# Transposes in two 64-row halves, w_out loaded in row order, and a new written-out order, in a fused attention and gated linear unit kernel

## The chip, the cores and the metric

The kernel runs on one core of one Trainium2 chip. A core has TensorE (PE: matmuls and transposes, which write to PSUM), VectorE (DVE), ScalarE (ACT), GpSimd (POOL) and SyncE (SP), which here does little but issue DMAs. The metric is the device time of one launch in microseconds. Before the change it is 201.42 us, the median of 3 runs (200.97 to 202.28).

## The reference

Inputs are q, k and v of 8 batches x 8 heads x 576 positions x 64, and three weights: w_val and w_out (512 x 512) and conv_w (5 x 512), all in float32. The output is 8 x 576 x 512 in float32.

```python
# attention, causal in blocks of 64
scores = (1/8) * q @ k.T
scores = where(block_i >= block_j, scores, -1e9)      # block = position // 64
attn = softmax(scores) @ v
x = attn.transpose(0, 2, 1, 3).reshape(8, 576, 512)   # heads side by side
# gated linear unit with a causal convolution over 5 positions
gate = sigmoid(sum_k conv_w[k] * x[:, s - 4 + k, :])
out = (gate * (x @ w_val)) @ w_out
```

## The kernel before

**Units of work.** Heads go in pairs: p = 0 to 31 is a pair of heads of one batch, four pairs a batch. A head's 576 positions are cut in 512 and a tail of 64; the tails of a batch's eight heads are loaded and turned together. For each pair:

- lq, lk, lv load q, k and v (v in one DMA for each head) as float32; cq and cv cast them to fp16, nearly always on POOL.
- T turns q and k: eight TensorE transposes of 128 x 128 into one PSUM bank; Te copies them to SBUF and puts the positions in order. lt, ct, TT and TTe do this for a batch's tails, and lvt, cvt load and cast the tails of v.
- S computes transposed scores in three pieces, t = 0, 1, 2. Each matmul has 64 rows (the size of a head), the two heads on different halves of the array, into two banks. E is the exponential on ACT, 128 x 1024 elements for each piece. mka and mkb clear the blocks that causality forbids, on POOL. SL and EL are the last tail's own scores, once a batch.
- A is attn times v, 30 matmuls of 128 rows and 65 columns (the 65th gives the sum); N divides by the sum on DVE.
- X turns the result, five transposes of 128 x 128, and Xe copies it to SBUF, so that a batch's x lies with its features on the partitions.

For each half batch n = 0 to 15, C is the convolution in 80 matmuls of 32 x 32, CS its tanh on ACT (a sigmoid in another form), V is x times w_val and Ve multiplies the two on DVE. For two batches u together, O projects 128 positions with w_out (t = 0 to 8), Oe copies a tile of the output to SBUF and Od stores it. The very last tile is done in two halves, OL, OLe, OLd.

**The weights.** w_val is cast with its columns permuted so that the features of V's output fall where the convolution's do. w_out has to match: lwo loads it, cwo casts it, W moves its rows in groups of 32 between partitions with 16 matmuls against a folded identity, and We copies them back with a factor of 0.5. CW turns conv_w with fp32 matmuls; CWe makes of it the diagonals that C uses.

**The order.** Nothing is scheduled by a compiler. The string PLAN (lines 12 to 101) lists all operations as name/indices/engine/bank, and the loop at its end issues them in this order. Each engine works through its own part of the list strictly in order, waiting on semaphores where an operand or a buffer isn't ready. S and G are the SP and POOL queues, P, V and A are TensorE, VectorE and ScalarE. So a load behind another load or an output store in PLAN is issued behind it, and a TensorE operation that has to wait holds all behind it.

**Buffers.** There are 5 tiles for loaded q and k and 5 for v, 4 each for cast and turned q and k, 5 for cast v, 4 for the exponentials, 6 for output tiles. PSUM's eight banks are three pairs (0 to 2: S, SL, A, C, V) and two single banks (3 and 4: T, TT, X, O and others). `mm` (line 127) records all matmuls, `copy` (lines 192 and 194) all copies and casts, so these lines gather many operations in the profile. Transposes are at line 322 (q and k), 354 (tails) and 453 (X).

Of the kernel before, what the change touches and what calls it, by code (L numbers as in the profile page):

```python
# [12 lines left out]
lk/1/S pact//A ppool//G lq/1/S lk/0/A lq/0/S lt/0.1/S pdve//V cq0/1/A w0/14/P/4 cq/1/G lt/0.0/S  # L13
lk/2/S lcv//S lq/2/S T/1/P/2 cq/2/G Te/1/A lq/3/S cq0/0/V lk/3/S S/1.0/P/2 lvt/0/S T0/1/P/3 E/1.0/A
T0e/1/V S/1.1/P/1 T0/0/P/0 lk/4/S T0e/0/A E/1.1/A lt/1.0/S lt/1.1/S S/0.1/P/0 cq/3/V lq/4/S ct/0/G
E/0.1/A S/0.0/P/1 TT/0/P/2 lv/0.0/S TTe/0/V E/0.0/A T/2/P/3 lv/0.1/S lq/5/S S/0.2/P/0 SL/0/P/2
Te/2/V S/1.2/P/1 T/3/P/4 Te/3/V lk/5/S lv/1.1/S CW//P/3 lv/1.0/S cvt/0/G cv/0/V E/0.2/A lk/6/S
lq/6/S E/1.2/A S/2.1/P/0 lv/3.1/S mka/0/G S/2.2/P/1 lvt/1/S ct/1/G TT/1/P/4 lv/2.0/S lv/3.0/S EL/0/A
mkb/1/G E/2.1/A S/3.0/P/2 CWe//V cq/4/G mkb/0/G A/0/P/0 TTe/1/V E/2.2/A N/0/V S/3.1/P/1 T/4/P/4
cq/5/G S/2.0/P/0 mka/1/G cv/1/G E/3.0/A E/3.1/A T/5/P/3 mkb/2/G lv/2.1/S cq/6/G S/3.2/P/1 E/2.0/A  # L20
Te/4/V lv/4.1/S mka/3/G E/3.2/A Te/5/V A/1/P/2 SL/1/P/0 S/4.1/P/1 EL/1/A T/6/P/3 N/1/V mka/2/G
cv/2/V lk/7/S S/4.0/P/0 X/0/P/4 cvt/1/G lwo/1/S mkb/3/G cv/3/G lv/4.0/S Te/6/V E/4.1/A S/4.2/P/2
E/4.0/A mka/4/G A/2/P/1 A/3/P/0 lwo/0/S E/4.2/A S/5.1/P/2 cwo/1/G N/2/V X/2/P/3 lq/7/S S/5.0/P/1
lv/5.0/S cv/4/G lv/5.1/S mkb/4/G Xe/0/A lwv/0/S lwv/1/S N/3/V E/5.1/A cq/7/G Xe/2/V lv/6.0/S
S/5.2/P/0 lv/6.1/S cv/5/G E/5.0/A X/3/P/4 Xe/3/V E/5.2/A X/1/P/3 lq/8/S A/4/P/2 lk/8/S Xe/1/V lk/9/S
N/4/V mkb/5/G C/0/P/1+0 CS/0.1/A T/7/P/3 S/6.0/P/2 X/4/P/4 lq/9/S CS/0.0/A lt/2.0/S S/6.2/P/0
cwo/0/G Te/7/V lt/2.1/S Xe/4/V E/6.0/A cwv/1/V lv/7.1/S S/6.1/P/1 E/6.2/A mka/5/G lv/7.0/S W/1/P/3
cwv/0/G E/6.1/A mka/6/G A/5/P/2 mkb/6/G We/1/A V/0.0/P/0 cv/6/G N/5/V cq/8/G cq/9/G S/7.1/P/1
W/3/P/3 W/2/P/4 Ve/0.0/V E/7.1/A lvt/2/S S/7.2/P/0 A/6/P/2 lk/11/S E/7.2/A S/7.0/P/1 ct/2/G W/0/P/0
lv/8.1/S We/2/V cv/7/G We/3/V lq/11/S E/7.0/A T/8/P/3 X/5/P/4 mka/7/G N/6/V Te/8/A lt/3.1/S lv/8.0/S  # L30
lk/10/S C/1/P/1+2 We/0/V S/8.1/P/0 Xe/5/V mkb/7/G TT/2/P/4 CS/1.0/A cq/11/G X/6/P/3 lq/10/S CS/1.1/A
V/0.1/P/1 E/8.1/A TTe/2/V lt/3.0/S Ve/0.1/V S/8.0/P/2 lv/12.0/S T/9/P/4 Xe/6/V E/8.0/A A/7/P/0
mka/8/G S/8.2/P/2 lk/12/S SL/2/P/1 O/0.0/P/3 Te/9/V O/0.1/P/4 EL/2/A E/8.2/A lq/13/S N/7/V cvt/2/G
lv/10.0/S S/9.1/P/0 S/9.2/P/1 mkb/8/G Oe/0.1/V Oe/0.0/A X/7/P/3 E/9.1/A Xe/7/V lv/11.1/S V/1.0/P/2
lv/9.1/S cv/8/G lv/9.0/S E/9.2/A Ve/1.0/V A/8/P/0 ct/3/G S/9.0/P/1 E/9.0/A T/11/P/3 lv/10.1/S
cq/10/G lt/4.1/S Te/11/A mkb/9/G T/10/P/4 lt/4.0/S N/8/V C/2/P/0+2 Te/10/V V/1.1/P/1 CS/2.0/A
lq/12/S S/10.0/P/0 Ve/1.1/V lt/5.1/S CS/2.1/A cv/9/G lq/16/S S/10.1/P/2 E/10.0/A lk/13/S E/10.1/A
TT/3/P/4 mka/9/G TTe/3/V lk/14/S S/10.2/P/1 mka/10/G cv/10/G O/0.3/P/3 E/10.2/A mkb/10/G lv/11.0/S
A/9/P/0 S/11.0/P/2 Oe/0.3/V lk/16/S N/9/V E/11.0/A S/11.1/P/1 lv/14.0/S cq/12/G O/0.2/P/4 A/10/P/0
lq/14/S lk/17/S Oe/0.2/V lv/13.0/S cq/13/G S/11.2/P/2 lq/15/S cv/11/G lv/12.1/S N/10/V T/12/P/3  # L40
lvt/4/S X/8/P/4 E/11.1/A C/3/P/1+0 E/11.2/A mkb/11/G cq/14/G Xe/8/A mka/11/G SL/3/P/2 CS/3.0/A
lvt/3/S Te/12/V EL/3/A CS/3.1/A X/10/P/4 Od/0.1/S lt/5.0/S T/13/P/3 V/2.1/P/1 lv/13.1/S S/12.1/P/2
Xe/10/V Te/13/V V/2.0/P/0 Ve/2.1/V V/3.0/P/1 X/9/P/4 lk/15/S Ve/2.0/V Ve/3.0/V E/12.1/A lv/15.0/S
lv/16.1/S A/11/P/0 S/12.0/P/2 lk/18/S N/11/V S/12.2/P/1 E/12.0/A cv/12/G Od/0.0/S E/12.2/A ct/4/G
O/0.5/P/3 cvt/3/G V/3.1/P/0 Xe/9/V TT/4/P/4 lk/19/S Oe/0.5/V T/14/P/3 S/13.0/P/2 Ve/3.1/V mkb/12/G
TTe/4/A E/13.0/A S/13.1/P/1 lv/15.1/S X/11/P/0 Od/0.2/S Te/14/V mka/12/G lv/16.0/S E/13.1/A
O/0.4/P/4 A/12/P/2 cq/15/G Oe/0.4/A Xe/11/V N/12/V cv/13/G S/13.2/P/0 S/14.0/P/1 mka/13/G O/0.6/P/3
T/15/P/4 E/14.0/A C/4/P/1+2 Oe/0.6/V E/13.2/A mkb/13/G X/12/P/3 cq/16/G CS/4.1/A A/13/P/0 SL/4/P/2
CS/4.0/A EL/4/A Te/15/V lv/14.1/S S/14.2/P/1 N/13/V lq/17/S E/14.2/A lv/18.1/S T/16/P/4 Xe/12/V
S/14.1/P/2 cv/14/G V/4.0/P/0 Ve/4.0/V E/14.1/A lvt/5/S mkb/14/G cv/15/G mka/14/G lq/18/S S/15.2/P/1  # L50
lq/20/S O/0.7/P/3 Oe/0.7/V Od/0.4/S E/15.2/A lv/17.1/S cvt/4/G Te/16/A lv/18.0/S A/14/P/0 S/15.1/P/2
E/15.1/A S/15.0/P/1 cq/17/G T/17/P/3 lq/19/S N/14/V E/15.0/A X/14/P/4 lt/6.1/S C/5/P/0+2 Te/17/V
S/16.1/P/1 O/0.8/P/3 lv/17.0/S cv/16/G CS/5.0/A CS/5.1/A mka/15/G mkb/15/G A/15/P/0 E/16.1/A cv/17/G
N/15/V cv/18/G V/4.1/P/2 Oe/0.8/A cq/18/G Xe/14/A X/13/P/3 lk/20/S Ve/4.1/V S/16.0/P/1 lq/21/S
S/16.2/P/0 lk/21/S E/16.0/A E/16.2/A ct/5/G X/15/P/4 V/5.0/P/2 Xe/15/V T/18/P/4 lt/6.0/S Od/0.3/S
S/17.0/P/1 Ve/5.0/V Xe/13/V mka/16/G lk/22/S mkb/16/G S/17.2/P/0 E/17.2/A A/16/P/2 E/17.0/A
O/1.1/P/3 lq/22/S S/17.1/P/0 N/16/V C/6/P/1+2 E/17.1/A mkb/17/G CS/6.0/A Oe/1.1/V lv/21.0/S
lv/20.1/S CS/6.1/A cq/19/G Te/18/V TT/5/P/3 V/5.1/P/0 S/18.1/P/1 Ve/5.1/V Od/0.7/S cq/22/G lv/19.0/S
lq/23/S S/18.2/P/2 lk/23/S cq/20/G lv/19.1/S TTe/5/A O/1.0/P/4 mka/17/G lv/22.0/S E/18.1/A Oe/1.0/V
T/19/P/0 E/18.2/A lv/20.0/S lv/21.1/S A/17/P/1 S/18.0/P/2 T/20/P/4 cq/21/G N/17/V X/16/P/3 Te/19/A  # L60
Te/20/V E/18.0/A lk/25/S Od/0.6/S ct/6/G SL/5/P/0 EL/5/A S/19.0/P/1 cvt/5/G V/6.0/P/2 S/19.2/P/0
mka/18/G mkb/18/G E/19.0/A Ve/6.0/V X/17/P/4 E/19.2/A lq/25/S S/19.1/P/1 Xe/16/V A/18/P/2 cv/20/G
E/19.1/A T/21/P/3 N/18/V lv/22.1/S cv/19/G Te/21/A C/7/P/0+1 CS/7.1/A lq/27/S V/6.1/P/2 lt/7.1/S
T/22/P/3 mkb/19/G S/20.1/P/1 CS/7.0/A Xe/17/V S/20.0/P/0 Ve/6.1/V E/20.1/A E/20.0/A S/20.2/P/2
Te/22/V E/20.2/A O/1.3/P/4 Od/0.5/S V/7.0/P/1 O/1.2/P/3 mka/19/G mka/20/G Oe/1.3/A lk/24/S lq/26/S
S/21.0/P/0 lv/25.0/S cq/25/G cv/21/G E/21.0/A lv/24.0/S Ve/7.0/V Oe/1.2/V lv/24.1/S S/21.2/P/1
# [38 lines left out]
def kernel(  # L105
# [32 lines left out]
    def consts(n, shape, dt, tag):  # L138
        return [const(shape, dt, f"{tag}_{i}") for i in range(n)]


    PP = [psum.tile([128, 2 if i < 3 else 1, 512], fp32, tag=f"P{i}", name=f"P{i}")
          for i in range(5)]

    def one(b):
        return PP[b][0:128, 0]

# [461 lines left out]
```

## Time and profile before

| what | us |
|---|---|
| median of 3 runs | 201.42 |
| the profiled execution: span, first to last instruction | 199.25 |
| TensorE busy | 184.3 |
| ScalarE busy | 139.4 |
| VectorE busy | 121.3 |
| GpSimd busy | 85.3 |
| last matmul ended | 195.6 |

The page gives only the span of the profiled execution; the time of a run also holds what lies around it, some 2.2 us if that execution was a median one. Times on the page are counted from the span's start. Busy time is the union of an engine's instructions. A matmul's recorded duration is its latency, so several overlap; the distance between starts tells what each costs. The loads and stores move 40.42 MB in 70,336 packets, of which 48,149 are under 512 bytes. The core's 16 DMA engines and the granted TensorE clock have rows of their own, 40 slices of about 5 us each.

### The profile page before, as it was taken

Reading aid. Unit: us, or ns where it says so; the run is one execution under the profiler, and the core shown is the slowest. Engines: PE = TensorE matmul, PEld = TensorE weight load, DVE = VectorE, ACT = ScalarE, POOL = GpSimd, SP = SyncE. Lnnn points to the kernel's source line nnn. Section 1 sums busy time; section 2 is a strip of 40 time slices with the busy share of each in tenths; the row PEclk is TensorE's granted clock in tenths of the full one; section 3 lists DMA queues with packets and bytes.
Section 4 is the critical chain, followed back from the end, with each engine's and each line's share of the span. In section 5 each row is a group of like instructions: output and inputs, shape, how many; then the busy total and the mean of one; then the engine's idle time right before and its main releaser. Section 6 shows DMA issues by size and latency. Waiting matters only on the chain.

```text
span 199.3 us, 8575 instructions
## 1 busy us (share of the span) xinstructions
PE 184.3 (92%) x3706; PEld 129.3 (65%) x3706; DVE 121.3 (61%) x193; ACT 139.4 (70%) x172; POOL 85.3 (43%) x201
## 2 busy tenths in 40 slices
PE   6389999699999799999999999999996999999992
PEld 3248677457676677767777776767764766676651
DVE  5047687675676676764666666777655383664562
ACT  3476896749779638798799888679694888643221
POOL 7255656763635535366394084282606041210000
PEclk9855899879999999999999999999999999999999
DMA  5999999999989999999969819991277610421445
GB/s 183 213 230 274 212 272 342 300 187 243 231 171 271 259 217 315 257 236 290 255 159 278 211 38 303 250 293 62 96 199 227 122 56 3 161 104 68 155 154 215
DMA packets 70336, 40.42 MB, mean 203 GB/s; under 512 B 48149, under 2 KB 64789, under 8 KB 70298
## 3 DMA queue, kind: packets, MB, share of 16 engines
q1 hardware_dynamic: 69882, 39.48, 77.6%
q8 instruction: 29, 0.48, 1.1%
q10 hardware_dynamic: 416, 0.39, 0.6%
q14 instruction: 9, 0.07, 0.1%
HBM read 30.42 MB, written 9.44 MB: 200 GB/s over the span
## 4 chain that ended last, share of the span: by engine, by line
PE 75%; DMA 9%; ACT 4%; POOL 4%; issue 3%; DVE 2%; SPq 1%; POOLq 0%; DVEq 0%; ACTq 0%
PE P L127 64%; PE P L322 7%; PE P L453 4%; DMA vs<-in_v_dram 3%; ACT pt L388 3%; DMA vts<-in_v_dram 3%; DMA qks<-in_q_dram 2%; PE P L354 1%; POOL qk L194 1%; DVE x L445 1%; ACT qkT L192 1%; POOL v16t L194 1%; POOL v L194 1%; POOL w_out L194 1%; POOL pt L410 0%
## 5 line engine op out<-in xcount | busy, mean ns | idle before, releaser
L388 ACT ACTIVATE pt<-P 128x1024 f16<-128x1024 f32 x96 | 93.7, 1025 | 24.0 <-PE P L127 22.9
L194 POOL CAST qk<-qks 128x1024 f16<-128x1024 f32 x30 | 31.0, 1043 | 15.4 <-DMA qks<-in_q_dram 10.9
L127 PE MATMUL P<-xt,w_val 128*128 128x288 f16 x256 | 37.3, 291 | 0.0
L127 PEld LDWEIGHTS <-pt 128*128 128x128 f16 x960 | 32.8, 99 | 5.9 <-issue 1.6
L127 PE MATMUL P<-v,pt 128*128 128x65 f16 x896 | 34.5, 196 | 1.9 <-POOL pt L410 0.9
L127 PE MATMUL P<-w_out,gv 128*128 128x512 f16 (+1 forms) x148 | 36.0, 374 | 0.0
L512 DVE SCALAR_TENSOR_TENSOR gv<-th,P 128x576 f16<-128x576 f32 x32 | 24.1, 752 | 18.9 <-PE P L127 15.0
L127 PE MATMUL P<-qkT 64*128 64x256 f16 (+3 forms) x256 | 31.8, 316 | 2.8 <-ACT qkT L192 1.8
L194 DVE COPY qkT<-P 128x1024 f16<-128x1024 f16 (+1 forms) x23 | 27.3, 1196 | 4.1 <-PE P L322 3.9
L127 PEld LDWEIGHTS <-w_val 128*128 128x128 f16 x256 | 23.8, 99 | 8.2 <-issue 1.1
L494 ACT ACTIVATE th<-P 128x576 f32<-128x576 f32 x32 | 19.2, 648 | 12.8 <-PE P L127 12.8
L127 PEld LDWEIGHTS <-qkT 64*128 64x128 f16 x512 | 17.0, 97 | 16.8 <-issue 10.0
L445 DVE TENSOR_TENSOR x<-P,rc 128x640 f16<-128x640 f32 x32 | 26.4, 824 | 1.1
L194 DVE COPY osb<-P 128x512 f32<-128x512 f32 x28 | 19.1, 688 | 10.4 <-PE P L127 8.3
L410 POOL MEMSET pt<- 64x256 f16 x32 | 9.8, 306 | 31.8 <-ACT pt L388 31.1
L322 PE MATMUL P<-ident,qk 128*128 128x128 f16 x256 | 20.8, 228 | 2.6 <-POOL qk L194 2.6
L444 DVE RECIPROCAL rc<-P 128x10 f32<-128x10 f32 x32 | 7.0, 220 | 25.0 <-PE P L127 23.7
L194 POOL CAST v<-vs 128x512 f16<-128x512 f32 x30 | 18.4, 619 | 8.3 <-DMA vs<-in_v_dram 5.0
L322 PEld LDWEIGHTS <-qk 128*128 128x128 f16 x256 | 16.1, 102 | 7.1 <-POOL qk L194 3.4
L127 PEld LDWEIGHTS <-gv 128*128 128x128 f16 x148 | 12.6, 98 | 12.2 <-issue 1.3
L127 PE MATMUL P<-xt,DG 32*32 32x288 f16 x1280 | 16.9, 288 | 0.0
L416 POOL MEMSET pt<- 64x128 f16 x32 | 6.5, 204 | 22.8 <-ACT pt L388 22.1
(57 smaller groups left out, 154.4 us busy)
## 6 DMA issues: line engine op xcount, KB each, us to landing
out_dram<-osb SPq DMA_DIRECT2D x35, 256.0 KB, 3.1
qks<-in_q_dram SPq DMA_DIRECT2D x32, 256.0 KB, 5.3
vs<-in_v_dram SPq DMA_DIRECT2D x64, 128.0 KB, 5.1
qks<-in_k_dram SPq DMA_DIRECT2D x31, 256.0 KB, 5.1
tls<-in_k_dram SPq DMA_DIRECT2D x8, 128.0 KB, 5.9
tls<-in_q_dram SPq DMA_DIRECT2D x8, 128.0 KB, 6.1
vts<-in_v_dram SPq DMA_DIRECT2D x8, 128.0 KB, 5.5
w_out_st<-in_moe_w_out_dram SPq DMA_DIRECT2D x2, 512.0 KB, 6.4
```

The source lines that it names most:

```text
L127: nc.tensor.matmul(out=out, lhsT=lhsT, rhs=rhs, start=start, stop=stop, skip_group_check=True)
L192: nc.scalar.copy(out=out, in_=in_)
L194: (nc.vector if eng == "V" else nc.gpsimd).tensor_copy(out=out, in_=in_)
L322: nc.tensor.transpose(out=r[:, o:o + 128], in_=t[0:128, c, 2 * i:2 * i + 2, 0:64], identity=ident16[0:128, 0:128])
L388: nc.scalar.activation(out=rot(pts, p)[0:128, 0:2, 512 * t:512 * t + 512], in_=PP[where.pop(("S", p, t))][0:128], func=AF.Exp, bias=0.0, s ...
L410: nc.gpsimd.memset(pt[64:128, 0:2, 0:1024].rearrange("p h (t s) -> p h t s", t=2)[:, :, :, 0:64], 0.0)
L416: nc.gpsimd.memset(rot(pts, p)[64:128, 0:2, 1024:1088], 0.0)
L444: nc.vector.reciprocal(out=rc[0:128], in_=r[:, :, :, 64:65])
L445: nc.vector.tensor_tensor(out=rot(x16, p)[0:128].rearrange("p i h d -> p h i d"), in0=r[:, :, :, 0:64], in1=rc[0:128].to_broadcast([128, 2 ...
L453: nc.tensor.transpose(out=half16(bank)[:, 128 * i:128 * i + 128], in_=rot(x16, p)[0:128, i, 0:2, 0:64], identity=ident16[0:128, 0:128])
L494: nc.scalar.activation(out=rot(ths, n)[0:128, 2 * i:2 * i + 2, 0:288], in_=PP[where["C", n][i]][0:128, 0:2, 0:288], func=AF.Tanh, bias=0.0 ...
L512: nc.vector.scalar_tensor_tensor(out=rot(gvs, b // 2)[0:128, 2 * y:2 * y + 2, b % 2, hf, 0:288], in0=rot(ths, n)[0:128, 2 * y:2 * y + 2, 0 ...
```

## The change

Four things change. Each transpose of 128 rows (T0, T, TT, X) becomes two of 64 rows, one for each head of the pair, with the same 128 columns of data as weights and a 64-column identity; the two halves go to the two banks of a pair. PSUM is now four pairs for all of these; O, CW, OL and the warm-up name a single bank, which is a half of a pair. The copies behind them read both banks; Xe copies 640 columns instead of 576.

w_out is loaded by four DMAs, each into 32 partitions, in the row order that the projection needs; cwo casts it with the factor 0.5, and W and We are gone. conv_w is cast to fp16 ahead of CW. The warm-up matmuls are 2 + 2 instead of 14. PLAN is a new list: it has another order on every engine, pairs of heads out of their numbers' order, and other engines for some copies (Oe: 28 on VectorE and 7 on ScalarE become 12 and 23; Xe: 21 and 11 become 28 and 4; cwo from GpSimd to VectorE; the last two OLe and OLd all on ScalarE).

```diff
-    PP = [psum.tile([128, 2 if i < 3 else 1, 512], fp32, tag=f"P{i}", name=f"P{i}")
-          for i in range(5)]
+    PP = [psum.tile([128, 2, 512], fp32, tag=f"P{i}", name=f"P{i}") for i in range(4)]

     def one(b):
-        return PP[b][0:128, 0]
-
-    def half16(b):
-        return one(b).bitcast(fp16)
+        return PP[b // 2][0:128, b % 2]
+
+    def both16(b):
+        return PP[b][0:128].rearrange("p r c -> p (r c)").bitcast(fp16).rearrange(
+            "p (r c) -> p r c", r=2)
...
     @op
-    def lwo(f, eng="S", bank=None):
-        DMA[eng].dma_start(out=w_out_st[0:128, 2 * f:2 * f + 2],
-                           in_=moe_w_out[256 * f:256 * f + 256].rearrange("(f p) n -> p f n", p=128))
+    def lwo(j, eng="S", bank=None):
+        DMA[eng].dma_start(out=w_out_st[32 * j:32 * j + 32, 0:4],
+                           in_=moe_w_out[128 * j:128 * j + 128].rearrange("(x i) n -> i x n", i=32))
...
     @op
     def cwo(f, eng, bank=None):
-        copy(eng, w_out_16[0:128, 2 * f:2 * f + 2], w_out_st[0:128, 2 * f:2 * f + 2])
+        o, i = w_out_sb[0:128, 2 * f:2 * f + 2], w_out_st[0:128, 2 * f:2 * f + 2]
+        if eng == "A":
+            nc.scalar.activation(out=o, in_=i, func=AF.Copy, bias=0.0, scale=0.5)
+        else:
+            nc.vector.tensor_scalar(out=o, in0=i, scalar1=0.5, scalar2=None, op0=ALU.mult)
+
+    @op
+    def ccv(eng, bank=None):
+        copy(eng, conv16[0:5, 0:512], conv_nat[0:5, 0:512])
+
+    def halves(r, o, x):
+        for h in range(2):
+            hs = slice(64 * h, 64 * h + 64)
+            nc.tensor.transpose(out=r[:, h, o:o + 64], in_=x[hs], identity=ident16[hs, hs])

     def transposes(t, i, r):
         for c in range(4):
-            o = 512 * i + 128 * c
-            nc.tensor.transpose(out=r[:, o:o + 128], in_=t[0:128, c, 2 * i:2 * i + 2, 0:64],
-                                identity=ident16[0:128, 0:128])
+            halves(r, 256 * i + 64 * c, t[0:128, c, 2 * i:2 * i + 2, 0:64])
...
     def X(p, eng, bank):
         where["X", p] = bank
         for i in range(5):
-            nc.tensor.transpose(out=half16(bank)[:, 128 * i:128 * i + 128],
-                                in_=rot(x16, p)[0:128, i, 0:2, 0:64],
-                                identity=ident16[0:128, 0:128])
+            halves(both16(bank), 64 * i, rot(x16, p)[0:128, i, 0:2, 0:64])

     def Xe(p, eng, bank=None):
         b, g = divmod(p, 4)
-        copy(eng, rot(xts, b)[0:128, g, 4:4 + SEQ], half16(where.pop(("X", p)))[:, 0:SEQ])
+        copy(eng, rot(xts, b)[0:128, g, 4:4 + 640].rearrange("p (i r s) -> p i r s", i=5, r=2),
+             both16(where.pop(("X", p)))[:, :, 0:320].rearrange("p r (i s) -> p i r s", i=5))
...
-            mm(one(bank)[:, 16 * g:16 * g + 5], conv_nat[0:5, 128 * g:128 * g + 128],
-               ident[0:5, 0:5])
+            mm(one(bank)[:, 16 * g:16 * g + 5], conv16[0:5, 128 * g:128 * g + 128],
+               ident16[0:5, 0:5])
...
-    def W(x, eng, bank):
-        where["W", x] = bank
-        rs = slice(32 * x, 32 * x + 32)
-        for j in range(4):
-            mm(one(bank)[32 * j:32 * j + 32, 0:512], idfold[rs, 0, 0:32], w_out_16[rs, j, 0:512])
```

The part of the new PLAN around the operation that the prediction speaks of most, T/22 (three lines of it):

```
S/21.1/P/3 lv/19.1/S lv/21.0/S mkb/18/G lk/22/S lq/24/S lv/22.1/S lt/7.0/S lv/21.1/S mkb/16/G
mka/19/G A/16/P/1 N/16/V EL/5/A TT/6/P/0 E/21.1/A cq/22/G T/22/P/2 TTe/6/V A/18/P/3 N/18/V
S/21.2/P/1 Te/22/A S/22.2/P/0 cv/19/G cv/21/G Od/0.3/S O/1.0/P/4 Oe/1.0/V E/21.2/A Od/0.6/S T/23/P/3
```

## The prediction

> **What bounds the kernel now.** I read the page's engine rows first, then its slices, then stretches of the span, then the instructions in order of time on TensorE, and last the DMA packets and the SP queue.
>
> ```profile
> span 199.3 us, 8575 instructions
> PE 184.3 (92%) x3706; PEld 129.3 (65%) x3706; DVE 121.3 (61%) x193; ACT 139.4 (70%) x172; POOL 85.3 (43%) x201
> ...
> PE   6389999699999799999999999999996999999992
> ...
> PEclk9855899879999999999999999999999999999999
> DMA  5999999999989999999969819991277610421445
> ```
>
> PE is the bound by share, but the last row says more: until 100 us, and with gaps until 134, the sixteen DMA engines are nearly full too. The stretches confirm it (columns: length, busy time of PE, PEld, DVE, ACT and POOL with counts, granted clock, DMA share, GB/s):
>
> ```profile
> 8.00:22.00 14.00, 12.28 (x126) 8.70 (x126) 6.21 (x9) 10.33 (x12) 6.77 (x13) 0.51 1.19 258
> ...
> 43.00:108.00 65.00, 63.77 (x1399) 46.12 (x1395) 42.77 (x67) 51.96 (x64) 34.19 (x72) 1.00 0.99 242
> 108.00:134.00 26.00, 25.98 (x597) 18.70 (x597) 17.51 (x28) 20.79 (x26) 12.94 (x28) 1.00 0.80 223
> ...
> 152.00:196.00 44.00, 43.59 (x857) 28.69 (x853) 25.86 (x41) 24.94 (x34) 6.14 (x20) 1.00 0.38 120
> ```
>
> From 43 to 108 us both are full; behind 108 only PE is. So a faster PE meets the loads, and I need the service time of both.
>
> PE, in order of time around 65 us:
>
> ```profile
> 64.78 0.28 PE L127 MATMUL P<-kt,qkT 64*128 64x64 f16 x8
> 64.99 0.62 PE L322 MATMUL P<-ident,qk 128*128 128x128 f16 x8
> 65.44 0.44 PE L453 MATMUL P<-ident,x 128*128 128x128 f16 x5
> 65.82 1.10 PE L127 MATMUL P<-xt,DG 32*32 32x288 f16 x80
> ```
>
> A matmul's recorded time is latency, so I use the distance between starts. Eight transposes to the next row: 0.45 us, 56 ns each. Eight 64-row matmuls with 64 columns take 0.28 us including one latency of 190 ns: 13 ns each, since the two halves run beside each other (in the whole trace 15 ns each, 30 a pair). From the last of these to the first transpose it is about 120 ns instead of 25: **a change between 128-row, 64-row and 32-row work costs 95 ns** (the same from the medians: 151 against 56 behind a transpose, 218 against 123 behind V, 311 against 216 behind O). The other spacings: A 30 x 29 ns = 0.88 us, V 8 x 123 = 0.98, O 4 x 216 = 0.86, C 0.89, one S about 0.22, T 8 x 56 = 0.45, X 0.28, TT 0.22.
>
> With these the old order sums to 173.3 us of PE, 165 changes (15.7 us) among it. The last matmul ended at 195.6, so PE lost 22.3 us: 9.5 before the first A at 20.5, 16.0 by A/10 at 63.6, only 6.3 more in the 132 us after that, 5% on the 125.7 us of work there (1.9 of it a wait for V's tail).
>
> The loads: the trace's packets take 21.5 ns (256 B, 45,056 of them), 58.6 ns (1 KB) and 93.9 ns (2 KB). Over 16 engines a q or k load of 256 KB costs 0.94 us, a v or tail load of 128 KB 0.69, an output tile 0.75, half a weight matrix 1.5. Summed in SP's order this gives 59.5 us at lk/13, and SP issued it by 59.2; 108.8 at lv/25.0, issued by 108.0. **The sum is the clock of the load queue until 108 us.** Casts that waited for a load began 3.6 to 4.7 us behind its sum. So before: T/13 (50.3 us of PE work ahead of it) needed 59.5 + 4.0 + 1.04 (cast) + 0.1 = 64.6, a lag of 14.3 behind the bare PE sum; the lag there was 16. The loads set the lag, PE the rest.
>
> **The change, part by part.**
>
> Transposes: 448 of 56 ns (25.1 us) become 896 halves. No row has a 64-row transpose. Ends: 15 ns a half, as the 64x64 score matmuls of the same shape (30 a pair, 11.6 us saved), or no overlap, 29 ns a half as the 65-column matmuls of A (58 a pair, 0.9 us lost). I take 15: same rows, columns and two output banks. The Trainium skill ("TensorE: Matmul & The Clock Gate", section "Wait — 56ns, not 53.3ns?") says that starts never come closer than about 25 ns however small N is, which speaks against this; the trace's 13 to 15 ns for these pairs disagree. By that rule a pair would cost 50, the time below 197.5 instead of 194.
>
> Changes of mode: T, TT and X now share S's mode; in the new order 140 changes are left, 25 fewer, 2.4 us. W falls away (0.9 us and a wait of 1.9 at 36 us), the convolution weights take one pass in fp16 instead of two (1.5 us to some 0.3), ten warm-up matmuls of 213 ns go (2.1, beside the first loads). New PE sum: **155.0 us**.
>
> Evacuations: Oe moves from DVE (28 to 12, 0.69 each) to ACT (7 to 23, 0.60), Xe the other way (ACT 11 to 4). ACT gains 9.5 - 4.5 = 5 us on 139, DVE loses about 8. Xe copies 640 elements for 576 in runs of 64: between 0.50 (by size from 0.452) and 0.76 (by size from Te's 1.219), at most 9 us on an engine 61% busy; beside PE. The two weight casts on DVE cost 0.69 to 1.46 each (its casts of 128x1024), in place of We's 2.7; once, beside loads. The new fp16 cast of the convolution weights is at most 0.43 (DVE's 128x512 copy), and CW stands behind it while loads are awaited.
>
> w_out: four DMAs of 256 KB into 32 partitions each for two into 128. Same bytes in the same 2 KB rows, 0.75 each, so no difference; if 32 partitions take twice as long, 3 us on every later load. The tails, into 64 partitions, show no such lag (3.0 to 6.6 us), so I take none.
>
> Order: this decides. PE's work ahead of a head is smaller, the loads ahead of it are not. The tightest place is T/22. Ahead of it and with it the queues issue 50 q and k loads (47.0), 62 v and tail loads (42.8), weights (6.0) and six output tiles (4.5): 100.3 us. T/22 can begin at 100.3 + 5.1 = **105.4**, with only 76.7 us of PE work ahead. A/20 gives nearly the same lag (112.0 + 4.5 with 88.2 ahead: 28.3 against 28.7). From T/22 on PE has 34 S (7.5), 14 A (12.3), 18 V (17.7), 9 C (8.0), 24 O and two half O (21.6), 10 T, 16 X, TT and SL (5.1) and 63 changes (6.0): 78.3 us. With before's 5% of loss 82.2, so PE ends at 187.6. Behind it before needed 3.65 us to the span's end; the last two copies and their DMAs are now all on ACT, where one waits for the other's issue: 4.1. **Span 191.7.** The median of the runs is 201.42, 2.2 above the profiled span of 199.25 (the page gives no other time of that execution); with the same 2.2 the time is **194** us, 3.7% faster. Of the 18 us that PE gains, some 11 are waited away for loads.
>
> SP's order also has outputs ahead of loads: Od/2.1 stands at a sum of 131.8 but needs O/2.1 near 140, and lv/28.1, lv/31.1 and lvt/7 stand behind it. Issued at 141, those are cast by 147; their users, A/31 and A/28, come at 154 and 161, so this costs nothing with 7 us of cover.
>
> **The rivals.**
>
> The loads are hidden after all, since DMA follows faster when PE frees buffers: PE then loses its old 22.3, 155.0 + 22.3 + 4.1 + 2.2 = 183.6. For it: DMA share is under 1 from 43 us. Against: SP's issue times track the sum within 1.2 us up to 108. Chance 0.15.
>
> The halves don't run in pairs: 164 of the pairs come from T/22 on, 28 ns each, 4.6 us more: 105.4 + 82.9 x 1.05 + 4.1 + 2.2 = 198.7. For it: no 64-row transpose is in the trace. Chance 0.13.
>
> **Slower: PSUM.** S had three bank pairs, T, X and O two banks of their own; now everything shares four pairs, and PE, in order, stands wherever a pair's last user isn't yet copied out. By holding time (matmul plus copy) the new demand is 412 us over four pairs, 103 of 190 us; before it was 313 over three, 104, so on average it isn't tighter. But each of the 130 operations from T/22 on can wait. Before, the loss behind A/10 is 6.3 us over 210 operations, 30 ns each; at 130 ns, 100 more, the forecast rises by 13 to 207. It is slower than before by 1% from 73 ns more. What speaks for it: ACT, 70% busy, now copies most outputs between exponentials of 1.03 us. Chance 0.14.
>
> Not priced apart: the granted clock. It was half from 8.0 to 21.7 and 38.7 to 42.2, where PE did only about 60% of its full-clock work; the new order has 25.3 us of work between A/0 at 21 and T/13, which its loads hold until 56, 72%. At half clock throughout that stretch PE would fall 8 us short, 3 of which the waits until T/22 absorb: 199. The Trainium skill (the same page, "Part 1: The HAM clock gate") lets the clock rise after about 3.4 us of busy PE; the trace shows it half for 13.7 us with PE recorded busy for 12.3 of 14.
>
> **How the numbers follow.** Forecast (190 to 198) 0.50, hidden loads 0.15, no pairs 0.13, PSUM 0.14, the clock or slow w_out loads (197 to 200) 0.08. The range 186 to 202 leaves out half of the hidden case and the PSUM case. One per cent (199.4 to 203.4) is about what a measurement of this kernel can tell from no change. Faster: 0.50 + 0.15 + most of 0.13 and half of 0.08, 0.76; same 0.10; slower 0.14.
>
> **What would show it.** Half transposes about 15 ns apart at L330; DMA share at 0.95 or more to about 125 us; PE standing for POOL's casts between 25 and 105 us, with T/22 near 105; from there PE full. I am wrong if T/22 comes much ahead of 105 (loads faster than their sum) or if PE, behind it, waits for ACT's and DVE's copies.

## The result, and the profile after

The changed kernel takes 213.73 us (median of 4 runs, 213.01 to 214.94) beside 201.19 us of the kernel before (199.58 to 202.28): 1.064 times as long, 95% interval 1.056 to 1.071. Forecast were 194.0 us and a range of 186 to 202. **It is slower by 12.5 us, where a gain of 7 was forecast.** Some runs of several kernels are over 1.5% longer than the fastest one of the same kernel; all times and ratios below leave these out, while two expectations name times with them in (205.2 and 208.9 us, here 203.34 and 207.16).

The page of the changed kernel, the same rows as were shown of before:

```profile
span 211.7 us, 9409 instructions
...
PE 171.2 (81%) x4124; PEld 115.5 (55%) x4124; DVE 115.4 (54%) x184; ACT 143.8 (68%) x180; POOL 83.8 (40%) x199
...
PE   2305877885798997979999995999999998979781
...
PEclk9999999999999999999999998899999999999999
DMA  5998979999999999997839889605618280112654
```

TensorE is busy for 171.2 us instead of 184.3, and its clock was granted nearly throughout (two slices with an 8; mean 0.99, before 0.96). But its row now has fives and sevens up to 65 us, and sevens and eights further on. Two of the same stretches of the span as before (length, busy time of PE, PEld, DVE, ACT and POOL with counts, granted clock, DMA share, GB/s):

```profile
43.00:108.00 65.00, 57.02 (x1473) 39.28 (x1474) 41.08 (x64) 49.23 (x59) 34.56 (x74) 1.00 0.99 230
108.00:134.00 26.00, 22.27 (x620) 15.24 (x613) 15.39 (x24) 18.95 (x24) 13.43 (x31) 0.93 0.90 244
```

From 43 to 108 us TensorE was busy for 63.8 us of 65, and now is for 57.0; from 108 to 134 for 22.3 of 26 instead of 26.0. The DMA row is much as it was. So TensorE has less to do and does it no sooner. The half-transposes themselves do what was expected. In order of time on TensorE:

```profile
49.74 0.41 PE L330 MATMUL P<-ident,qk 64*128 64x64 f16 x16
49.99 0.31 PE L330 MATMUL P<-ident,x 64*128 64x64 f16 x10
50.13 0.38 PE L127 MATMUL P<-qkT 64*128 64x384 f16 x4
```

From the first of the 16 halves to the first of X it is 0.25 us, and the ten of X take 0.14 us up to the next row: 14 to 16 ns a half. Over the whole trace the mean distance within an operation is 14.6 ns for T and 14.3 for X (medians of the operations).

What TensorE waited for, by the view of waits (us in all, times, longest), before and then after:

```profile
PE P L322 <- POOL qk L194: 2.6, 1, 2.6
PE P L127 <- ACT qkT L192: 1.8, 2, 1.1
PE P L127 <- issue: 1.5, 1, 1.5
```

```profile
PE P L127 <- issue: 8.7, 9, 2.6
PE P L330 <- DVE qk L194: 7.5, 2, 7.1
PE P L127 <- ACT osb L192: 4.2, 5, 1.3
PE P L127 <- DVE qkT L194: 3.4, 5, 1.4
...
PE P L330 <- ACT pt L396: 2.1, 5, 0.8
PE P L127 <- DVE osb L194: 1.9, 4, 0.8
```

The first line of the second list is the one to look at. **"issue" means that the engine waited for nothing the profile shows**: no semaphore, no buffer, no operand. It went from 1.5 us in one piece to 8.7 us in nine. Next come waits for operands (the first cast of q and k, Te on DVE) and behind them the waits for output copies on ACT and DVE, of which the list before has none.

One number carries the comparison: the **lag**, the start of a TensorE operation minus the TensorE work ahead of it (prediction, first part).

| lag in us at | before | after | more |
|---|---|---|---|
| A/0 | 9.5 | 19.6 | 10.1 |
| A/10 | 16.0 | 31.8 | 15.8 |
| T/22 | 19.1 | 38.1 | 19.0 |
| A/29 | 21.1 | 46.7 | 25.6 |
| the end | 22.3 | 53.1 | 30.8 |

The work became 18.3 us less, the lag 30.8 us more: that is the 12.5 us by which the last matmul came later (195.6 and 208.1 us). I put each piece of the lag to what ended last: a bank not yet copied out 5.4 us before and 17.8 after, an operand 8.1 and 15.4, "issue" 3.2 and 10.4. These pieces cover 16.7 of the 22.3 us and 43.6 of the 53.1. The attribution is worked out from the trace; that each of them matters is for the experiments.

Of the waits for output copies (ACT osb, DVE osb) 4.4 us lie behind 187 us, in five pieces. So the lag rises by 6.4 us behind A/29, where it rose by 1.2 before.

### The profile page after: what moved, and what is told of

Same layout as the page of the kernel before. It is cut to its first block, busy times and chain, and to the rows that moved or that the text cites. A ratio compares the mean times of both kernels' runs of the same rounds, so it can differ in the third digit from the quotient of the medians.

```text
span 211.7 us, 9409 instructions
## 1 busy us (share of the span) xinstructions
PE 171.2 (81%) x4124; PEld 115.5 (55%) x4124; DVE 115.4 (54%) x184; ACT 143.8 (68%) x180; POOL 83.8 (40%) x199
## 4 chain that ended last, share of the span: by engine, by line
PE 58%; DMA 12%; ACT 10%; DVE 9%; issue 8%; SPq 1%; POOL 1%; ACTq 0%; DVEq 0%; POOLq 0%
PE P L127 53%; ACT pt L396 5%; PE P L330 5%; DMA out_dram<-osb 4%; DMA qks<-in_k_dram 4%; ACT osb L192 2%; DVE qkT L194 2%; DMA vs<-in_v_dram 2%; DVE osb L194 2%; DVE x L453 2%; DMA conv_nat<-in_moe_conv_w_dram 1%; ACT th L501 1%; DVE gv L519 1%; SPq L207 1%; SPq L229 1%
## 5 line engine op out<-in xcount | busy, mean ns | idle before, releaser
L194 POOL CAST qk<-qks 128x1024 f16<-128x1024 f32 x29 | 30.4, 1052 | 28.1 <-DMA qks<-in_q_dram 10.0
L127 PE MATMUL P<-qkT 64*128 64x128 f16 (+3 forms) x256 | 33.9, 318 | 4.5 <-DVE qkT L194 3.4
L127 PE MATMUL P<-xt,w_val 128*128 128x288 f16 x256 | 35.4, 287 | 0.3 <-ACT osb L192 0.2
L194 DVE COPY qkT<-P 128x1024 f16<-128x1024 f16 (+1 forms) x23 | 27.5, 1200 | 11.1 <-PE P L330 9.6
L501 ACT ACTIVATE th<-P 128x576 f32<-128x576 f32 x32 | 19.2, 650 | 10.5 <-PE P L127 10.3
L192 ACT COPY osb<-P 128x512 f32<-128x512 f32 x23 | 13.4, 589 | 17.9 <-PE P L127 12.0
L127 PEld LDWEIGHTS <-qkT 64*128 64x128 f16 x512 | 16.5, 97 | 16.0 <-issue 9.8
L194 POOL CAST v<-vs 128x512 f16<-128x512 f32 x30 | 18.3, 618 | 14.1 <-DMA vs<-in_v_dram 5.2
L418 POOL MEMSET pt<- 64x256 f16 x32 | 9.8, 306 | 35.2 <-ACT pt L396 33.7
L127 PE MATMUL P<-xt,DG 32*32 32x288 f16 x1280 | 18.5, 292 | 6.1 <-issue 5.1
L330 PE MATMUL P<-ident,qk 64*128 64x64 f16 x512 | 14.1, 199 | 11.2 <-DVE qk L194 7.5
L330 PEld LDWEIGHTS <-qk 64*128 64x128 f16 x512 | 11.5, 100 | 16.6 <-DVE qk L194 7.9
L127 PEld LDWEIGHTS <-DG 32*32 32x32 f16 x1280 | 12.1, 88 | 12.9 <-issue 10.4
```

The costliest lines, as they stand in the source:

```text
L127: nc.tensor.matmul(out=out, lhsT=lhsT, rhs=rhs, start=start, stop=stop, skip_group_check=True)
L192: nc.scalar.copy(out=out, in_=in_)
L194: (nc.vector if eng == "V" else nc.gpsimd).tensor_copy(out=out, in_=in_)
L330: nc.tensor.transpose(out=r[:, h, o:o + 64], in_=x[hs], identity=ident16[hs, hs])
L418: nc.gpsimd.memset(pt[64:128, 0:2, 0:1024].rearrange("p h (t s) -> p h t s", t=2)[:, :, :, 0:64], 0.0)
L501: nc.scalar.activation(out=rot(ths, n)[0:128, 2 * i:2 * i + 2, 0:288], in_=PP[where["C", n][i]][0:128, 0:2, 0:288], func=AF.Tanh, bias=0.0 ...
```

## What "issue" is

The clearest place is at 127 us, in the middle of a convolution (TensorE's rows in order of time):

```profile
126.56 0.86 PE L127 MATMUL P<-xt,DG 32*32 32x288 f16 x64
130.05 0.35 PE L127 MATMUL P<-xt,DG 32*32 32x288 f16 x16 [2.62 <-issue]
130.33 0.57 PE L330 MATMUL P<-ident,qk 64*128 64x64 f16 x16
...
133.14 1.08 PE L127 MATMUL P<-xt,DG 32*32 32x288 f16 x62
134.60 0.42 PE L127 MATMUL P<-xt,DG 32*32 32x288 f16 x18 [0.38 <-issue]
```

C/8 issues 64 of its 80 matmuls, stands for 2.6 us, and then issues the other 16. The 16 need nothing that the 64 did not have: same operands, same banks. C/9 is cut behind 62. In the groups by line and shape the convolution before and after is:

```profile
L127 PE MATMUL P<-xt,DG 32*32 32x288 f16 x1280 | 16.9, 288 | 0.0
```

```profile
L127 PE MATMUL P<-xt,DG 32*32 32x288 f16 x1280 | 18.5, 292 | 6.1 <-issue 5.1 <-ACT pt L396 0.5 <-DVE osb L194 0.4
```

The columns are busy us, mean ns | idle us ahead of them, by releaser: no idle time before, 5.1 us of "issue" after.

The trace also has packets of 16,384 bytes on a queue of the kind "instruction": 29 before, 32 after. TensorE has 7,424 and 8,259 recorded instructions, since each matmul is two, a weight load and the matmul itself; 256 in a packet gives 29.0 and 32.3. So I numbered TensorE's instructions in the trace and listed the gaps over 0.35 us that end shortly behind the end of such a packet:

```
after:  instruction  packet ended  it started  gap (us)
        1217 (C)         42.44        43.74      0.61
        1473 (A)         47.51        49.11      1.96
        1729 (A)         54.80        56.16      1.15
        2241 (C)         64.80        66.36      0.95
        3521 (A)         92.69        94.17      1.05
        5057 (C)        128.50       130.05      2.91
        5313 (C)        132.93       134.60      0.67
        5569 (C)        137.60       138.98      0.72
        7361 (C)        175.37       176.90      0.97    sum 11.0
before:  961 (W)         36.45        38.06      1.86
        2241 (S)         66.48        68.05      1.42    sum  3.3
```

Every number is 193 + 256 k. **TensorE stands where a block of its instructions begins that has just arrived**, and goes on 1.3 to 1.7 us behind the packet's end. Below, a stand means such a gap, and its length is the distance between two starts as in the last column. The packet of the next block starts when the last one is entered, mostly 1.5 to 2.9 us later while the DMA engines are full of loads (up to 4.6), and takes 0.9 to 2.3 us. From one block to the next these eleven times took 3.8 to 7.1 us. Where TensorE would have got through a block's 128 matmuls in less, it stood. A convolution issues 80 in 0.76 us (9.5 ns each), a turned pair of heads 16 or 10 at 14 to 15 ns, so dense stretches of these run out of instructions.

## The experiments

The theories: **L**, loads hold TensorE, as the prediction has it; **H**, the half-transposes cost more than they save; **P**, TensorE waits for bank pairs that are not yet copied out; and later **F**, its instructions come too late. Ratios are against the kernel before, run on the same chip.

**1. Transposes and order, apart.** Three kernels keep the operations of the kernel before in its order on each engine, without W and We, with w_out in row order and conv_w cast first, and with banks given anew by the order in which they come free. `old_small` has whole transposes in any single bank, `old_128_pairs` whole transposes that hold a pair each, `old_halves` the changed code. `new_128` is the changed kernel with whole transposes in the first bank of a pair:

```diff
 def halves(r, o, x):
-    for h in range(2):
-        nc.tensor.transpose(out=r[:, h, o:o + 64], in_=x[hs], identity=ident16[hs, hs])
+    nc.tensor.transpose(out=r[:, 0, 2 * o:2 * o + 128], in_=x, identity=ident16)
```

> The kernel before with the small parts of the change alone: w_out by four loads in row order with no W and We, conv_w cast to fp16 first, the old order on every engine, transposes whole, in any of the eight banks (each operation takes the bank or pair that comes free first). Theory P (bank pairs: PE loses its time waiting for a pair that is still being copied out): transposes take one bank, so nothing gets tighter; the removed wait of 1.9 us and the 2.3 us of PE work show, 197 to 200. Theory O (the new order itself loses the time): the same, 197 to 200. Theory H (the half transposes lose it): the same.

> As the run with the old order and small parts, but each whole transpose reserves a pair, as the halves do, though it writes one bank of it. Theory P: 206 to 215, about like the halves in the old order, since the reservation is the cause and not the halves. Theory O: 198 to 201, as pairs cost nothing. Theory H: 198 to 201.

> The code after the change with the old order on every engine; only the choice among the four pairs is made anew (earliest free). Theory P: T, X and TT now hold a pair each, 5 places become 4, so bank waits like those after the change, 206 to 213. Theory O: the old order keeps its lag and PE gains up to 11 us, of which the loads eat about half: 190 to 197. Theory H: as slow as after the change, 210 to 214.

> The changed kernel with its order and its pairs untouched, but every transpose whole again, in the first bank of its pair. Theory P: PE has 11.6 us more work, part of which lies in the time that it waits anyway: 213 to 220. Theory O: the same, 213 to 220. Theory H: the loss goes with the halves, 198 to 204.

Measured: 218.43 us (ratio 1.089, 1.080 to 1.097) for `old_small`, 219.12 (1.092) for `old_128_pairs`, 218.33 (1.092) for `old_halves` and 217.55 (1.083, 1.073 to 1.093) for `new_128`. Against `new_128` the changed kernel's 213.73 shows that in its own order the half-transposes save some 4 us, so H falls as far as their time goes; what the second bank costs is the same in both and isn't in this comparison. The three in the old order missed all that was expected of them, and they tell less than meant: the banks were given out for other durations than those on the chip, and VectorE stood at the cast of w_out until the loads had landed (X/2 waits 5 us for it at 37 us). Two cleaner kernels follow from that.

**2. The small parts alone.** `before_small` is the kernel before with its exact banks and order; only lwo (four), cwo (on VectorE, where We stood), ccv ahead of CW, and no W.

> The kernel before, its banks and its order kept to the letter, with the small parts of the change alone: four loads of w_out in row order, W and We gone, the two casts of w_out at the places of two of the We on DVE, conv_w cast first. It differs from the run of the old order with small parts (218.4) in the banks, which there were given anew, and in the place of w_out's casts on DVE. If the small parts are harmless and the banks or the place cost those 17 us: 197 to 201. If the loads of w_out into 32 partitions are themselves the cause: 210 or more.

Measured: 204.36 us, ratio 1.017 (1.008 to 1.025): slower, where 2.3 us of busy TensorE had gone (182.0 for 184.3). In the trace CW begins at 19.2 us instead of 16.6. By A/13 the two kernels are level (it begins at 82.69 and 82.78 us), so the work saved had been waited away. Then, in the middle of A/13:

```profile
82.69 0.23 PE L126 MATMUL P<-v,pt 128*128 128x65 f16 x2
84.91 0.52 PE L126 MATMUL P<-v,pt 128*128 128x65 f16 x12 [2.00 <-issue]
```

Two matmuls, 2.0 us of nothing, the other 28: a stand for instructions. Behind it the granted clock was 0.66 from 85 to 90 us (columns as in the result's stretches):

```profile
85.00:90.00 5.00, 5.00 (x76) 3.51 (x75) 1.52 (x4) 2.54 (x3) 2.01 (x6) 0.66 0.99 277
```

A/14 begins at 90.92 us instead of 87.41, 3.6 us later against A/13 than before: 2.2 are the stand, and the other 1.4 go with the slow clock. All that this kernel loses in its trace arises here. This line led to theory F.

**3. Loads and the start.** `after_light` and `before_light` move a quarter of the columns of q, k and v in each load, from a buffer's second use on (the results of these pairs are then made of older data). `after_start` issues lk/1 and lq/1 on SP behind those of pair 0, not on ACT.

```diff
-lq/1/A ... lk/1/A                       # behind cq0 and T0e on ACT
+lk/0/S lq/0/S lk/1/S lq/1/S
```

> The changed kernel, where from a buffer's second use on each load of q, k and v moves a quarter of its columns (the rest of the tile holds older data): the DMA work falls by about 80 us, everything else stays. Theory L (late loads and SP's standing behind buffers set the lag): PE's 155 us with the start's 20 us and few waits, 180 to 192. Theory P (waits for bank pairs and the copies behind them): the loads were not what PE waited for after the start, 203 to 212.

> The same reduction of the loads in the kernel before. If the loads set its lag, as the prediction has it: PE's 173 us and a lag of 10 to 15 instead of 22, 190 to 196. If not: 199 to 202.

> The changed kernel with one edit in its order: the q and k loads of pair 1 go out on SP right behind those of pair 0 instead of on ACT, where the second stood behind three other operations until 6.3 us and landed at 14.6. If the lost start (10 us more lag at the first A than before) is carried to the end: 203 to 208. If later waits would have taken that time anyway (loads, banks): 210 to 214.

Measured: 207.16 us for `after_light` (a single run); 193.50 for `before_light`, ratio 0.963 (0.952 to 0.974); 212.26 for `after_start`, ratio 1.054 (1.042 to 1.065). Lighter loads take 7.7 us from the kernel before and 6.6 from the changed one: L is no cause of the difference. Nor is it loads alone that this measures, since the stands fell with them, from 11.0 to 6.7 us and from 3.3 to 1.2: the page counts the packets of instructions among those of the same 16 engines. The start of the changed kernel is late, which these lines show (load issued, cast, transposes of pair 1):

```profile
6.26 0.39 ACTq L207 DMA_DIRECT2D qks<-in_k_dram  x1
...
14.71 0.69 DVE L194 CAST qk<-qks 128x1024 f16<-128x1024 f32 x1 [8.03 <-DMA qks<-in_k_dram]
...
15.46 0.61 PE L330 MATMUL P<-ident,qk 64*128 64x64 f16 x16 [7.13 <-DVE qk L194]
```

The load of k for pair 1 is issued at 6.26 us and cast at 14.71, and T/1 waited for 7.1 us. With it on SP, A/0 began at 22.7 us instead of 26.0, though TT/0 then waited 3.9 us for the tails' cast. Yet only 1.5 us were gained at the end, no more than the runs scatter.

**4. Fewer instructions.** `after_fewer` and `before_fewer` change C alone:

```diff
-for kk in range(5):
+for kk in range(3):
-    mm(PP[bank[row // 2]][cs, row % 2, 0:288], DG[...], rot(xts, b)[rs, g, kk + 288 * hf:kk + 288 * hf + 288], ...)
+    mm(PP[bank[row // 2]][cs, row % 2, 0:480], DG[...], rot(xts, b)[rs, g, kk + 96 * hf:kk + 96 * hf + 480], ...)
```

> The trace fetches TensorE's instructions in packets of 16,384 bytes, 256 instructions (each matmul is two). TensorE stands nine times in front of an instruction whose number is 193 + 256 k and starts it 1.3 to 1.7 us behind the end of such a packet: 11.0 us in the changed kernel, two times and 3.3 us before. Here C adds three taps instead of five and each of its matmuls has 480 columns instead of 288: 48 x 480 = 80 x 288, so the same columns pass through TensorE with 1,024 instructions fewer in all (leaves out two taps, and the columns that the longer matmuls add come from other positions). Theory F (instructions come too late): the stands fall from 11.0 to under 5 us and the time by 4 to 7 us, to 206 to 209. Theory P (only the waits for bank pairs count): same time within 1.5 us, 212 to 215.

> The same edit of C in the kernel before (three taps of 480 columns for five of 288, leaves out two taps). Theory F: its two stands of 3.3 us go, the time falls by 0 to 3 us, to 198 to 201, less than in the changed kernel. Theory P: no change.

Measured: **203.34 us (two runs), ratio 1.011 (1.000 to 1.022)**, and 196.99, ratio 0.978 (0.970 to 0.987), both below what was expected. The stands fell from 11.0 to 1.9 us and from 3.3 to 1.1. The DMA row of the page of `after_fewer` (span 202.4 us), and its convolution by line and shape:

```profile
DMA  5999979999999999899979949927508181021654
```

```profile
L127 PE MATMUL P<-xt,DG 32*32 32x480 f16 x768 | 14.5, 370 | 1.0 <-DVE osb L194 0.5 <-ACT pt L396 0.5
```

The idle time of "issue" ahead of C is gone, and the DMA row holds its nines longer: with TensorE ahead, loads are asked for sooner. Not all of the 10.4 us are stands. 48 matmuls go out in 0.52 us where 80 took 0.76, so that C with the columns of its last round is about 0.16 us shorter, 2.6 us over 16; the expectation had it as equal. The kernel before got shorter by 4.2 us, the same 2.6 and 1.6 more. So taking the stands away is worth about 7.8 us to the changed kernel and 1.6 to the one before: **some 6 of the 12.5 us**, by the three intervals give or take 3, and the largest gain of any single edit.

`before_shift72` and `before_shift40` put 72 and 40 matmuls of one column behind the warm-up, in idle time, so that other instructions stand at 193 + 256 k.

```diff
+for _ in range(72):
+    mm(one(bank)[:, 0:1], wz[0:2, 0:128], wz[0:2, 0:1])
```

> The kernel before with 72 matmuls of one column behind the warm-up, where TensorE is idle before the first loads land (about 2 us of 3 idle ones). Nothing else changes, but each later instruction's number grows by 144, so that other instructions stand at 193 + 256 k. With the times of the trace before, and 5 us from one such instruction to the next at the least (4.6 behind 112 us, 4 behind 150), the stands come to 7.8 us instead of 5.0 by the same sum: near 46, 60, 86, 104 and 117 us in place of 38 and 68. Theory F: stands there, the time is 0 to 4 us longer, 201 to 206. Without it: no stands at these places, no change.

> The same with 40 such matmuls, 80 instructions: by the same sum 2.7 us of stands, near 35 us and small ones behind it. Theory F: 0 to 3 us shorter than before, 198 to 201.5; without it no change.

Measured: 199.48 us, ratio 0.991 (0.987 to 0.995), for 72; for 40 the six runs lie between 196.37 and 201.30, too wide to tell 1%. The stands at 38 and 68 us were gone and others came, again at 193 + 256 k: 1.34 us at 35.8, 0.48 at 46.0, 1.14 at 84.7 and 1.37 at 114.5 with 72; 1.15 at 35.2, 1.03 at 86.5 and 1.81 at 92.7 with 40. That the places follow the numbers is what F says; three of the four with 72 lie within 3 us of places worked out, and two such places (60 and 104 us) show none. Their sum was missed (4.3 and 4.0 us for 7.8 and 2.7), and the time did not follow the sum: with 72 the kernel is 0.9% faster, within what was called no change. Part of a stand in this kernel may be time that a later wait takes anyway, and the early matmuls may do something for the start; which it is stays open. So this pair shows where stands fall, and not what they cost.

**5. Faster copies.** `after_halfexp` and `before_halfexp` let E cover half of its columns from a buffer's second use on. The other two do the same for Te, Xe, Oe and Ve as well, on top of the shorter C.

```diff
-nc.scalar.activation(out=...[0:128, 0:2, 512 * t:512 * t + 512], in_=PP[...][0:128], func=AF.Exp, ...)
+nc.scalar.activation(out=...[0:128, 0:2, 512 * t:512 * t + 256], in_=PP[...][0:128, 0:2, 0:256], func=AF.Exp, ...)
```

> The changed kernel in which, from a buffer's second use on, each exponential covers 256 of 512 columns of each head (leaves out half of the exponentials; E takes some 0.6 us instead of 1.03), so that a bank pair of S comes free 0.4 us earlier and ACT is freer for the copies. Of TensorE's waits for bank pairs, 17.8 us without the stands for instructions, 7.8 end with E and 1.6 with Oe on ACT. Theory P: most of these go, the time falls by 6 to 10 us, to 204 to 208. Theory F (instructions alone): at most 2 us, 211 to 214, since a denser TensorE stands for its instructions more.

> The same halving of the exponentials in the kernel before (leaves out half of them), where 2.6 us of TensorE's waits end with E: 198 to 201 by either theory. If it gains as much as in the changed kernel, the copies did not become tighter through the change.

> The changed kernel with three taps of 480 columns in C for five of 288 (205.2 us, hardly a stand for instructions left), and in it, from a buffer's second use on, the exponentials, Te, Xe, Oe and Ve cover half of their columns (leaves out two taps and half of these results), so that bank pairs are copied out sooner. Theory P: what is left of the loss is waits for pairs behind copies; most of them go and the time is 195 to 201. If it is the late start and the loads: 202 to 205.

> The same two edits in the kernel before (197.0 with the first alone). It has few waits for banks, so 194 to 197 by either theory; the distance between the two kernels, 8.2 us with the stands alone taken away, then is 0 to 5 by theory P and stays at 7 or more if the copies are not the cause.

Measured: 209.99 us, ratio 1.044 (1.035 to 1.052), against 200.80, ratio 1.004 (0.997 to 1.011): faster exponentials are worth 3.7 us to the changed kernel and nothing to the one before, though less than P alone would have it; 9.9 us of stands were still there. With all copies halved and the shorter C: 199.66, ratio 0.998 (0.993 to 1.003), against 194.25, ratio 0.967 (0.960 to 0.974). Halving the copies took 3.7 us more from the changed kernel and 2.7 from the other. The distance between the two kernels was 6.4 us with the shorter C and is 5.4 with halved copies too (6.5 and 6.2 by the ratios). So slow copies cost both kernels much the same once the stands are gone, and their part in the difference, 1.0 us at the most, can't be told from the scatter. In the traces of this last pair A/0 still begins at 24.6 and 19.8 us: the late start is still there.

**6. The half-transposes alone.** `before_halves` is the kernel before, its list and banks unchanged, but T0, T, TT and X go in halves into banks 3 and 4 taken as one pair. Three copies had to move ahead by a place or two, since otherwise two engines wait for each other (Xe/14, Xe/13, Te/18).

```diff
-PP = [psum.tile([128, 2 if i < 3 else 1, 512], ...) for i in range(5)]
+PP = [psum.tile([128, 2, 512], ...) for i in range(4)]       # T0, T, TT, X: PP[min(bank, 3)], both halves
```

> The kernel before with the half-transposes alone: T0, T, TT and X turn in two 64-row halves into a bank pair, which is the old single banks 3 and 4 taken together; all other banks, weights, and the order of TensorE, GpSimd and SyncE are as before (three copies had to move ahead by one place or two on ScalarE and VectorE). By the spacings TensorE has some 14 us less work, 418 matmuls more (836 instructions), and nowhere to put a second transpose while the first is copied. If the halves are worth what they save: 188 to 196. Theory F and P (instructions, and one pair in place of two banks): the stands for instructions grow from 3.3 to 5 to 9 us, the waits for bank pairs by 4 to 10 us, the time is 199 to 208. If it comes near the changed kernel's 213.7, the new order is not to blame.

Measured: **255.14 us, ratio 1.268 (1.259 to 1.277)**, far outside of every case (the halves are 448 matmuls more, not 418). Its page, and what TensorE waited for:

```profile
span 253.5 us, 9475 instructions
...
PE 188.8 (74%) x4154; PEld 127.8 (50%) x4154; DVE 121.7 (48%) x193; ACT 141.2 (56%) x172; POOL 84.9 (33%) x201
```

```profile
PE P L322 <- DVE qkT L194: 14.3, 10, 2.3
PE P L127 <- DVE qkT L194: 8.6, 6, 2.3
PE P L322 <- DVE xt L194: 6.2, 7, 1.6
PE P L127 <- ACT qkT L192: 5.5, 4, 2.1
```

TensorE is idle for 64.7 us of 253.5; before it was 15.0 of 199.3. It stands at transposes, and at the output matmuls that use a bank of that pair, for copies of the transposes before them on DVE and ACT (qkT, xt). Stands for instructions are only 1.1 us here. A whole transpose of q and k fills one bank, so that the next could go to the other while the first is copied for 1.2 us; a pair of halves takes both. Part of the 54 us is the clock: it was at half for 34 us of this trace and for 17 before. The rest is the price of the half-transposes where one pair stands in for two banks. It is not a price of the halves as such: `old_halves`, with all operations spread over four pairs, took no longer than `old_small` with whole transposes (218.33 and 218.43).

**7. Stands and loads together.** `after_fewer_light` has the shorter C and the lighter loads.

> The changed kernel with both: three taps of 480 columns in C for five of 288 (leaves out two taps), and loads of q, k and v that from a buffer's second use on move a quarter of their columns. Alone, the first gave 205.2 and the second 208.9 of 213.7. If loads and stands for instructions cover for each other, both together give more than the sum: 194 to 199. If they are independent: 200 to 201. If what is left is waits for bank pairs and the late start: 201 to 205.

Measured: 198.12 us, ratio 0.986 (0.979 to 0.993). The time lies where causes that cover for each other were expected, but together the two edits take 15.6 us, alone 10.4 and 6.6, the sum 17.0. So nothing shows that they cover for each other. They overlap, since lighter loads alone take 4.2 us of the stands; with both edits the trace has none left.

## Why the prediction was wrong, point by point

The forecast put the end of TensorE's work at 187.6 us, 155.0 of work and 32.6 of lag; measured were 208.1. All 20.5 us are lag. Up to T/22 it is 9.4 us over the forecast (38.1 for 28.7), 5.7 of them stands for instructions; behind T/22 11.1 over (15.0 for 3.9), 5.3 of them stands.

1. **The spacings** (56, 30 for a pair of halves, 95 for a change): right. At 14 to 15 ns a half the pairs gain what was forecast, and `new_128` confirms the direction. The floor of 25 ns between starts, which the prediction cites from the Trainium skill ("TensorE: Matmul & The Clock Gate", section "Wait — 56ns, not 53.3ns?"), does not hold for these pairs. But the step priced a matmul by time alone. Each is also two instructions, and "896 halves" is 896 more of those than 448 transposes. With whole transposes the new order has 7.6 us of stands (`new_128`), with halves 11.0.
2. **"The loads set the lag, PE the rest", with T/22 at 105.4**: the step that failed. The term that was mis-sized is 100.3, the sum of packet times taken for the time at which the load of T/22 is issued. It was issued at 109.6, and the way from there to T/22 took the 5.1 us of the forecast (5.2):

```profile
102.17 0.75 SPq L207 DMA_DIRECT2D qks<-in_q_dram  x1
106.01 0.62 POOL L194 CAST v<-vs 128x512 f16<-128x512 f32 x1 [4.08 <-DMA vs<-in_v_dram]
106.56 0.62 POOL L194 CAST tl<-tls 128x512 f16<-128x512 f32 x1
107.21 0.61 SPq L229 DMA_DIRECT2D tls<-in_k_dram  x1
...
109.62 0.51 SPq L207 DMA_DIRECT2D qks<-in_k_dram  x1
113.70 1.04 POOL L194 CAST qk<-qks 128x1024 f16<-128x1024 f32 x1 [1.56 <-DMA qks<-in_k_dram]
114.80 0.41 PE L330 MATMUL P<-ident,qk 64*128 64x64 f16 x16
```

SP was behind its sum, 9.3 us here. 4.3 of them arose in one piece: SP stood from 102.9 to 107.2 at lt/7.1 until ct/5 had read that tile, and ct/5 stood on POOL behind cv/16, which waited for a load issued at 99.7. The rest came in smaller pieces from 53 us on, which I did not trace back one by one. So the load queue was held by buffers freed late, and not only by what the DMA engines can move: with a quarter of the bytes (`after_light`) T/22 still began at 111.0. The sum is only a bound. The kernel before had shown that too: T/13, which the sum lets begin at 64.6, began there at 68.57 and not at the 66.3 that a lag of 16 gives, 3.3 us behind the end of its cast; a stand of 1.4 us lay just ahead of it.
3. **The start**: A/0 was taken to stay at 21 us and came at 26.0. The waits that the new order adds there (T/1 for a load issued on ACT, 7.1 us) were not priced at all. `after_start` shows that undoing this one wait gives 1.5 us at the end, though A/0 came 3.3 us earlier; whether the rest of the late start is carried to the end was not settled.
4. **"Evacuations ... beside PE", Oe to ACT at nothing**: wrong. TensorE waited 4.2 us for ACT's output copies and 1.9 for DVE's, where the list before shows none; most of it behind 187 us. It is what the prediction named as a sign of being wrong. An engine that is 68% busy is no hidden engine when a bank pair hangs on it.
5. **The rival PSUM** (0.14) named a real part of the mechanism and its place, but not enough of it. Behind T/22 what is left without stands is 9.7 us over 130 operations, 75 ns each, 45 more than before; the rival wanted 100 and decided from 73. By itself it would have made the forecast 200, no loss. "By holding time ... it isn't tighter" compared means of pair use. What counts is that a transpose now takes two banks at once, and `before_halves` puts 54 us on that where nothing else is given more room.
6. **What no part of the prediction had**: instructions. The Trainium skill ("Runtime: NRT & Kernel Launch", section "Instruction fetch mechanics") says that an engine's instructions arrive in blocks of 16 KiB, 256 of them, by a DMA queue of its own, and that the cost of crossing a block is mostly hidden. The packets and the places 193 + 256 k agree with the blocks; hidden they were not, with 11.0 us of stands. The number of instructions alone does not make the stands: `new_128` has 7,363 recorded on TensorE, fewer than the kernel before, and 7.6 us of stands, while `before_halves` has 8,319 and 1.1. How fast TensorE gets to the next block, and how full the DMA engines are then, changes with the order. The trace before had the sign: one wait of 1.5 us for "issue" in its list, inside W, which the prediction took for a wait of W's own and credited to the change when W went.
7. **The other rivals**: hidden loads and unpaired halves are out. The clock, feared for 8 us, was granted nearly throughout. It was half only from 130.4 to 133.8 us, right behind the longest stand; an estimate from the like stretch of `before_small` is 1.4 us. The tail was 3.6 us for 4.1, and 2.0 us lay around the span for 2.2.

So there is no single cause. By experiment the stands are some 6 us of the difference, give or take 3 (7.7 by the trace, part of which might have been waited anyway), the copies 1.0 at the most, and over 5 us stay that I could not split between the late start, the loads and the remaining waits for pairs. No version tried is faster than the kernel before by over 1% without leaving work out.

## What to carry to other kernels

Look at the supply of instructions beside time: a gap of 1 to 3 us that the profile calls "issue", in the middle of an operation and at a fixed distance in instructions, is the sign that a block came late. It comes where many short matmuls stand close together while loads fill the DMA engines; splitting an operation in two that take half as long makes such stretches denser, and an order can do so without one instruction more. When an operation starts to take two banks at once, price it by what can no longer be in flight beside it, not by mean use. And a sum of transfer times says when a load can be issued at the earliest; in a new order, check for each buffer who frees it, and behind what that one stands.

## What the runs showed of the hardware that was not expected

- TensorE's instructions come in packets of 256. From entering one block to starting the next it took 3.8 to 7.1 us where TensorE stood for it, longest where the DMA engines were full; it went on 1.3 to 1.7 us behind the end of the packet. With a quarter of the load bytes the stands fell from 11.0 to 6.7 us.
- 32-row matmuls of 288 columns go out 9.5 ns apart, of 480 columns 10.9 ns: their time follows their number more than their columns (80 in 0.76 us, 48 with as many columns in all in 0.52).
- The 2.0 us stand in `before_small` was followed by 3.4 us at half clock, which went with 1.4 us of time. The same shows in five more traces: a half-clock stretch of 3.4 us begins within 1.2 us of the end of a stand of 1.9 to 2.9 us (at 38.7 us before, 130.4 after, 132.4 in `after_halfexp`, 69.1 in `before_halfexp`, 133.9 in `after_start`). Other stands as long have none behind them, as that of 1.96 us at 49.1 after. That the stand lowers the clock was not tested.
